# Weight sign by a leaky slope, pinned decay operands, one v tile, gl on GpSimd and fewer early quanta in a fused attention and feed-forward kernel

## The chip, the cores and the metric

The kernel runs on one core of one Trainium2 chip. The metric is the device time of one execution in microseconds (us). The core has TensorE (PE in the profile; PEld is its weight load), VectorE (DVE), ScalarE (ACT), GpSimd (POOL) and SyncE (SP), which here issues every DMA. Each engine works through its own queue in order; semaphores tie the queues together.

## The reference, cut to what matters

```python
scores = scale * np.matmul(q, k.transpose(0, 1, 3, 2))      # 8 batches, 8 heads, 576 tokens, D = 64
cum = np.cumsum(np.log(np.clip(f, 0.0001, 1.0)), axis=-1)
scores = np.where(causal, -1e9, scores + cum[:, :, :, None] - cum[:, :, None, :])
attn = softmax(scores)                                      # with 1e-9 added to the sum
x = np.matmul(attn, v)  # heads side by side: 4608 tokens x 512
h = x @ w_in            # 512 x 2048, float64 weights
g = np.maximum(0.01 * h, h)
out = (g @ w_out).astype(np.float32)
```

So it is causal attention with a forget gate (a decay that is added to the scores), and behind it a feed-forward layer with a leaky ReLU over all 4608 tokens.

## The kernel before, in words

**Precision.** The matmuls of the feed-forward layer and most of the attention run on pairs: a number is rounded to the matmul type (the high part, names ending in h), and the rest is kept as a low part (l). A product is three matmuls: high by high, high by low, low by high.

**Weights.** They lie in memory as float64. `load_weight` (line 157 on) takes one of 16 pieces, 128 partitions by 1024 numbers, as pairs of 32-bit words. ScalarE scales the high word's magnitude with `Abs` (L166); VectorE shifts it left by three (L167), puts the sign back with an AND and an OR (L168), and adds the scaled low word (L172); ScalarE rounds to the high part (L176), VectorE makes the low part (L177). Two raw buffers take turns, and the DMA of piece n+2 is asked for between L172 and L176.

**Early steps.** Before the loop over heads come 13 steps, x = 0 to 12. Twelve of them treat the first 256 tokens of batches 0 to 2, two heads at a time (four steps a batch). `early_scores` makes scores, masked minimum on VectorE (L296 or L326), exponential on ScalarE (L300 or L330) and the scaling by the inverse sum; `early_values` of the step before transposes the weights on PE (tre, L349), copies them by ScalarE (pte, L353) and multiplies by v (ave, L355 and L356). The decays enter the scores by a matmul of `pick`, which selects a head, with `both`, the decays of the two row blocks (L279, L318). `pick` comes from `ident_r`, a copy of the identity. In steps 0 to 3 idle `warm` matmuls on zeros (L114) stand between the scores. WQ says how many weight pieces have been treated by each step: one a step up to step 7, then two. At step 4 (LATER) `later_decays` makes the decays of the full heads (scan L215, L218, L222, ScalarE casts L227, GpSimd subtractions) and writes them to DRAM.

**Quanta.** The feed-forward work is a generator, `ffn`. It goes through 18 groups of 256 tokens. For each group and each of eight weight parts p it makes h (PE, L581, in two halves), g by ScalarE (`Prelu`, L588), gh by VectorE (L594) and gl by VectorE (L595), and one part later the output matmuls (L616, in two halves). Each half is one quantum, so a part has four quanta and a group 32. Groups 0 and 1 are done in two halves of the weights. `fill(n)` takes n quanta from it; it stops where tokens or weight pieces are not there yet. FQ says how many quanta an early step takes. A group's tokens are fetched to `xs`, rounded by VectorE to `xh` and subtracted by GpSimd (helper `minus`, L139), either at part 5 of the group before, if the fetch was made by then, or right where the group begins.

**Heads.** After the early steps, `fix` sets up tiles that stay, and the loop over 64 heads begins: the full 576 tokens of batches 3 to 7, then the rest of batches 0 to 2. In each turn t the head's scores (L425) are interleaved with the transposes (L452) and values (L494) of head t-1 and with fills. `split(t + 1)` makes the next head's operands: ScalarE rounds q and k (L393, L394), GpSimd subtracts for the low parts (s and fixed_m2a or fixed_m2b), VectorE rounds v in two casts (the four full chunks from `vm`, L403; the last 64 tokens from `vt`, L405) and GpSimd subtracts twice for v's low part. A turn's quanta follow from `step = min(have / (left + SLACK), MAXQ) / 8`, with `have` the quanta of ready tokens that are not done, and `left` the turns until more tokens are ready. Behind the heads, the last `fill` does what is left.

**Order.** The code's order is not that of the engines: a scheduler sorts the instructions of each engine by priority and its own estimate of when operands are ready, and lets ready ones overtake. `tc.keep_in_program_order(ins)` adds an edge so that `ins` is queued behind the instruction that was traced before it on its engine; others may still overtake both.

Of the kernel before, what the change touches and what calls it, by code (L numbers as in the profile page):

```python
# [26 lines left out]
GHA = ()  # L27
LATER = 4
ONV = (1, 3)
# [3 lines left out]
ZE = (("z0", "z1", "z2", "z3"), ("vm", "s2b", "m2b", "s2a"))  # L33
FQ = (0, 0, 0, 0, 0, 8, 8, 8, 8, 8, 8, 8, 8)
BUFS = dict(ost=2)
# [7 lines left out]
def forgetting_attention_ffn(ctx, tc, qT, kT, v4, vr, f, w_in, w_out, out):  # L43
# [75 lines left out]
    ident_r = one.tile([P, P], F32R, name="ident_r")  # L119
    nc.vector.tensor_copy(ident_r, eye)  # L120
    ident = ident_r.bitcast(F32)
# [16 lines left out]
    def minus(out, a, b):  # L138
        nc.gpsimd.tensor_tensor(out, a, b, op=ALU.subtract)  # L139
# [17 lines left out]
    def load_weight(n):  # L157

        loaded.append(n)
        _, wh, wl = wpieces[n]  # L160
        wh, wl = (w.rearrange("p c f -> p (c f)") for w in (wh, wl))
        raw = raws.pop(n).rearrange("p m w two -> p (m w) two")
        lo, hi = raw[:, :, 0], raw[:, :, 1]
        t = one.tile([P, 8 * P], I32, tag="vs", name=f"wt_{n}")
        tf = t.bitcast(F32)
        nc.scalar.activation(tf, hi.bitcast(F32), AF.Abs, scale=REBIAS)  # L166
        nc.vector.tensor_scalar(t, t, 3, None, op0=ALU.logical_shift_left)  # L167
        nc.vector.scalar_tensor_tensor(  # L168
            t, hi, -0x80000000, t, op0=ALU.bitwise_and, op1=ALU.bitwise_or
        )  # L170
        low = t.bitcast(U16).rearrange("p (w two) -> p w two", two=2)[:, :, 0]
        nc.vector.scalar_tensor_tensor(  # L172
            low, lo.bitcast(U32), 0.937 * 2.0**-29, low, op0=ALU.mult, op1=ALU.add
        )
        ask(n + 2)
        nc.scalar.copy(wh, tf)  # L176
        nc.vector.tensor_tensor(wl, tf, wh.bitcast(F32), op=ALU.subtract)  # L177
# [8 lines left out]
    pick = one.tile([P, NHEAD], F32R, tag="vt", name="pick")  # L186
    both = one.tile([P, P + T], F32R, tag="kraw", name="both")
    decay_r = [both[:, :P], both[:, P:P + T]]
    bounds = ((0, E), (E, S))

    def decays():
# [7 lines left out]
        )  # L199
        nc.vector.tensor_tensor(pick, ident[:, :NHEAD], ident[:, NHEAD:], op=ALU.add)  # L200
        d = one.tile([P, P + T], F32, tag="z3", name="d")
        for i in range(2):
# [5 lines left out]
        nc.scalar.copy(both, d)  # L208
        nc.vector.tensor_tensor(
            both[NHEAD:], d[NHEAD:], both[NHEAD:].bitcast(F32), op=ALU.subtract  # L210
        )

    def later_decays():

        nc.vector.tensor_tensor_scan(  # L215
            fc[:, E:], fr[:, E:], fr[:, E:], fc[:, E - 1:E], op0=ALU.add, op1=ALU.bypass
        )
        nc.vector.tensor_scalar(fc, fc, -1.0 / SCALE, None, op0=ALU.mult)  # L218
# [16 lines left out]
    def load(t):  # L235
# [8 lines left out]
        if s % 2 == 0:  # L244
            g = s // 2
            nf = min(c1, NFULL)
            vm = one.tile([P, 2, NFULL, D], F32, tag="vm", name=f"vm_{t}")
            nc.sync.dma_start(vm[:, :, :nf], v4[g][:, :, :nf])
            vt = None
            if c1 == NCH:  # L250
                vt = one.tile([REST, 2, D], F32, tag="vt", name=f"vt_{t}")
                nc.sync.dma_start(vt, vr[g])
            pairs[s // 2, c0] = dict(vm=vm, vt=vt)

# [113 lines left out]
    def fix():  # L368
# [11 lines left out]
        vs = fixed["vs"] = one.tile([P, 2, NCH, 2 * D], F32R, tag="vs", name="fixed_vs")  # L380
        nc.gpsimd.memset(vs[:, :, NFULL].bitcast(F32), 0.0)

    def split(t):
# [18 lines left out]
        vs = fixed["vs"][:, o]  # L402
        nc.vector.tensor_copy(vs[:, :NFULL, :D], p["vm"][:, o])  # L403
        minus(vs[:, :NFULL, D:], p["vm"][:, o], vs[:, :NFULL, :D].bitcast(F32))
        nc.vector.tensor_copy(vs[:REST, NFULL, :D], p["vt"][:, o])  # L405
        minus(vs[:REST, NFULL, D:], p["vt"][:, o], vs[:REST, NFULL, :D].bitcast(F32))

# [149 lines left out]
    def ffn():  # L557
# [4 lines left out]
        for at, (n, p0, p1) in enumerate(order):  # L562
# [9 lines left out]
            for p in range(p0, p1):  # L572
# [20 lines left out]
                else:  # L593
                    nc.vector.tensor_copy(gh, g)  # L594
                nc.vector.tensor_tensor(gl, g, gh.bitcast(F32), op=ALU.subtract)  # L595
                yield True
# [39 lines left out]
    quanta = ffn()  # L636
    ready, used, credit = [0], [0], [0.0]

    def fill(n):

        credit[0] += n
        while credit[0] >= 1:
            credit[0] -= 1
            if not next(quanta, None):
                credit[0] = 0
                return
            used[0] += 1
# [22 lines left out]
    ask(1)  # L670
    decays()
    for x, (b, g) in enumerate(steps + [(NE, 0)]):
        if x + 2 < len(steps):
            early_load(*steps[x + 2])
        if x < len(steps):
            early_scores(b, g)
            weights(sum(WQ[:x + 1]))
        if x == LATER:
            later_decays()
        if x:  # L680
            early_values(*steps[x - 1])
            if steps[x - 1][1] == HPB // 2 - 1:
                ready[0] = (steps[x - 1][0] + 1) * T
        fill(FQ[x])
    fix()
    load(0)
    split(0)
    for t in range(nt + 1):
# [25 lines left out]
        if t + 1 < nt:  # L714
            split(t + 1)
        fill(step * (3 - len(spans(t - 1)) if t else 1))
    fill(NG * NQ)

# [33 lines left out]
```

## Time and profile before

| | |
|---|---|
| median of three runs | 1211.28 us (1211.24 to 1211.35) |
| the profiled execution | 1210.85 us |
| its span, first to last instruction | 1209.0 us |
| mean granted TensorE clock | 0.994 |
| busy: PE, DVE, ACT, POOL | 1187.2, 720.5, 610.1, 296.7 us |
| DMA moved | 110.50 MB, mean 91 GB/s |

The profile is of one execution. Its page gives busy time of each engine and groups of instructions by line; other views of the same trace give who waited for whom, the instructions in order of time, the chain of work that ended last, and busy times within stretches that one names. A row of the timeline is start, duration, engine, line, operation, tiles (out<-in), and in brackets the idle time before it and what ended that. A row of the waits is who waited for whom, the sum in us, how often, and the longest. A row of groups ends in busy us, mean ns of one, and the idle time before. PEclk is the share of its full clock that PE was granted.

### The profile page before, as it was taken

Reading aid. Unit: us, or ns where it says so; the run is one execution under the profiler, and the core shown is the slowest. Engines: PE = TensorE matmul, PEld = TensorE weight load, DVE = VectorE, ACT = ScalarE, POOL = GpSimd, SP = SyncE. Lnnn points to the kernel's source line nnn. Section 1 sums busy time; section 2 is a strip of 40 time slices with the busy share of each in tenths; the row PEclk is TensorE's granted clock in tenths of the full one; section 3 lists DMA queues with packets and bytes.
Section 4 is the critical chain, followed back from the end, with each engine's and each line's share of the span. In section 5 each row is a group of like instructions: output and inputs, shape, how many; then the busy total and the mean of one; then the engine's idle time right before and its main releaser. Section 6 shows DMA issues by size and latency. Waiting matters only on the chain.

```text
span 1209.0 us, 21922 instructions
## 1 busy us (share of the span) xinstructions
PE 1187.2 (98%) x7876; PEld 1053.5 (87%) x7876; DVE 720.5 (60%) x1821; ACT 610.1 (50%) x1467; POOL 296.7 (25%) x295
## 2 busy tenths in 40 slices
PE   9899999999999999999999999999999999999998
PEld 6677888898999999999999999999999989888997
DVE  6898767775666666665665555535454666663221
ACT  6775556664565555555554544434434455552111
POOL 0000233332322323232323222223122433330000
PEclk9899999999999999999999999999999999999999
DMA  6544333433233322323232313122213233321000
GB/s 208 180 150 152 117 106 107 124 108 104 80 97 98 115 80 80 98 87 96 70 92 88 115 55 102 38 91 58 83 50 93 76 89 105 91 72 46 19 18 18
DMA packets 69677, 110.50 MB, mean 91 GB/s; under 512 B 10368, under 2 KB 35184, under 8 KB 69568
## 3 DMA queue, kind: packets, MB, share of 16 engines
q1 hardware_dynamic: 69568, 109.09, 29.5%
q8 instruction: 63, 1.03, 0.4%
q14 instruction: 46, 0.38, 0.1%
HBM read 82.62 MB, written 18.56 MB: 84 GB/s over the span
## 4 chain that ended last, share of the span: by engine, by line
PE 90%; DVE 3%; ACT 3%; issue 2%; POOL 1%; DMA 0%; DVEq 0%; ACTq 0%; POOLq 0%
PE h L581 32%; PE o L616 31%; PE sc L425 8%; PE av L494 7%; PE tr L452 7%; PE warm L114 1%; PE ave L355 1%; POOL xs L139 1%; PE tre L349 1%; PE sce L317 1%; ACT wt L166 0%; DVE wt L172 0%; DVE gl L595 0%; PE ave L356 0%; PE sce L287 0%
## 5 line engine op out<-in xcount | busy, mean ns | idle before, releaser
L581 PE MATMUL h<-xh,win_h 128*128 128x256 f32 x1152 | 327.4, 285 | 0.0
L581 PE MATMUL h<-xh,win_l 128*128 128x256 f32 x1152 | 323.6, 281 | 0.4 <-DVE win_l L177 0.4
L581 PE MATMUL h<-xs,win_h 128*128 128x256 f32 x1024 | 287.6, 281 | 5.7 <-POOL xs L139 5.7
L139 POOL TENSOR_TENSOR s<-qraw,s 64x576 fp32r<-64x576 f32 (+1 forms) x64 | 82.0, 1280 | 657.1 <-ACT s L393 597.9
L616 PE MATMUL o<-wout_h,gh 128*128 128x512 f32 x576 | 231.8, 402 | 0.0
L616 PE MATMUL o<-wout_l,gh 128*128 128x512 f32 x576 | 228.6, 397 | 0.0
L616 PE MATMUL o<-wout_h,gl 128*128 128x512 f32 x576 | 227.8, 396 | 0.1
L581 PEld LDWEIGHTS h<-xh,win_h 128*128 128x128 f32 x1152 | 217.5, 189 | 5.6 <-issue 0.5
L581 PEld LDWEIGHTS h<-xh,win_l 128*128 128x128 f32 x1152 | 217.2, 189 | 0.7 <-DVE win_l L177 0.6
L581 PEld LDWEIGHTS h<-xs,win_h 128*128 128x128 f32 x1024 | 193.2, 189 | 10.5 <-POOL xs L139 7.0
L588 ACT ACTIVATE g<-h 128x512 f32<-128x512 f32 x144 | 85.9, 597 | 226.9 <-PE h L581 225.0
L465 ACT CAST ph<-tr 128x128 fp32r<-128x128 f32 (+2 forms) x272 | 121.7, 450 | 133.3 <-PE tr L452 129.8
L594 DVE CAST gh<-g 128x512 fp32r<-128x512 f32 x144 | 74.9, 520 | 188.6 <-ACT g L588 186.0
L467 DVE TENSOR_TENSOR pl<-tr,ph 128x128 fp32r<-128x128 f32 (+2 forms) x272 | 138.4, 516 | 31.3 <-ACT ph L465 30.8
L616 PEld LDWEIGHTS o<-wout_h,gl 128*128 128x128 f32 x576 | 108.2, 188 | 25.6 <-issue 0.5
L425 PE MATMUL sc<-m,s 128*128 128x128 f32 (+2 forms) x336 | 121.8, 367 | 1.8 <-POOL s L139 1.5
L616 PEld LDWEIGHTS o<-wout_h,gh 128*128 128x128 f32 x576 | 108.4, 188 | 16.8 <-DVE ql L273 0.2
L616 PEld LDWEIGHTS o<-wout_l,gh 128*128 128x128 f32 x576 | 108.5, 188 | 16.1
L436 ACT ACTIVATE fixed_z<-fixed_z,max 96x480 f32<-96x480 f32 (+1 forms) x128 | 94.3, 736 | 46.2 <-DVE max L430 44.7
L430 DVE CUSTOM_DVE_ANT_0 z<-sc,tri 128x128 f32<-128x128 f32 (+1 forms) x144 | 63.4, 443 | 88.9 <-PE sc L425 88.1
L430 DVE CUSTOM_DVE_ANT_0 fixed_z<-sc,tri 96x480 f32<-96x480 f32 (+1 forms) x128 | 70.4, 550 | 63.2 <-PE sc L425 62.2
L595 DVE TENSOR_TENSOR gl<-g,gh 128x512 fp32r<-128x512 f32 x144 | 102.3, 710 | 3.1
(131 smaller groups left out, 1871.1 us busy)
## 6 DMA issues: line engine op xcount, KB each, us to landing
kraw<-in_kT SPq DMA_DIRECT2D x128, 144.0 KB
qraw<-in_qT SPq DMA_DIRECT2D x80, 144.0 KB
wraw<-in_w_in SPq DMA_DIRECT2D x16, 512.0 KB
wraw<-in_w_out SPq DMA_DIRECT2D x16, 512.0 KB
vm<-in_v SPq DMA_DIRECT2D x32, 256.0 KB
xs<-xd SPq DMA_DIRECT2D x16, 512.0 KB
out<-ost SPq DMA_DIRECT2D x28, 256.0 KB
rb<-inv SPq DMA_DIRECT2D x40, 144.0 KB
```

What stands on the lines that cost most here:

```text
L139: nc.gpsimd.tensor_tensor(out, a, b, op=ALU.subtract)
L425: nc.tensor.matmul(ps[:m, :b - a], h["s" + w][:, cols], h["m" + w][:, a:b], start=y == 0, stop=y == 1,)
L430: nc.vector.tensor_tensor_reduce(out=z[:, a:b], in0=ps[:m, :b - a], in1=tri[:m, at:at + b - a], scale=-SCALE, scalar=3.0e38 if x == 0 else ...
L436: nc.scalar.activation(z, z, AF.Exp, bias=h["max"][:m, last:last + 1], scale=-1.0, accum_out=fixed["sum" + "ab"[s // 2 % 2]][:m, i, s % 2: ...
L452: nc.tensor.transpose(ps[:, x * m:(x + 1) * m], z[:m, j * P:(j + 1) * P], ident[:m, :m])
L465: nc.scalar.copy(o, src)
L467: nc.vector.tensor_tensor(o, src, hi.bitcast(F32), op=ALU.subtract)
L494: nc.tensor.matmul(ps[:, a - lo:hi - lo], fixed["vs"][:, odd, j, :], h[w][:, at:at + hi - a], start=(n == 0), stop=(n == len(steps) - 1),)
L581: nc.tensor.matmul(ph[:, e, :], w[:, c, fs], xx[:, c, :], start=(c == 0 and x == 0), stop=(c == NCC - 1 and x == 2),)
L588: nc.scalar.activation(g, ph, AF.Prelu, alpha=0.01)
L595: nc.vector.tensor_tensor(gl, g, gh.bitcast(F32), op=ALU.subtract)
L616: nc.tensor.matmul(acc[k], gg[:, e, ts], w[:, e, :], start=(fc_ == 2 * p0 and x == 0), stop=(fc_ == 2 * p1 - 1 and x == 2),)
```

## The change

It has five parts.

- The sign: `Abs` becomes `Prelu` with slope -(2^32) for negative numbers. A negative number thus gets a positive result whose exponent is 32 higher, and the shift by three moves that bit to the place of the sign. The AND and OR (L168) goes.
- The decays: the copy to `ident_r`, `pick` (now traced ahead of `decays`), the subtraction into `both` and the scan of the later decays are kept in program order. `later_decays` comes at step 0 instead of 4.
- Step 4: the values of step 3 are traced ahead of the scores of step 4, not behind.
- v: `vm` is one tile that stays, with five chunks, the last one zero below the 64 tokens; ScalarE rounds all of it in one copy, GpSimd subtracts once.
- Quanta: the early steps 5 to 8 take 4 and steps 9 to 12 take 5, instead of 8. In the loop over heads gl is made by GpSimd instead of VectorE; before and behind it stays on VectorE.

```diff
-LATER = 4
+LATER = 0
+FIRST = (4,)
...
-FQ = (0, 0, 0, 0, 0, 8, 8, 8, 8, 8, 8, 8, 8)
+FQ = (0, 0, 0, 0, 0, 4, 4, 4, 4, 5, 5, 5, 5)
...
-    nc.vector.tensor_copy(ident_r, eye)
+    tc.keep_in_program_order(nc.vector.tensor_copy(ident_r, eye))
...
-        nc.scalar.activation(tf, hi.bitcast(F32), AF.Abs, scale=REBIAS)
+        nc.scalar.activation(tf, hi.bitcast(F32), AF.Prelu, scale=REBIAS, alpha=-(2.0**32))
         nc.vector.tensor_scalar(t, t, 3, None, op0=ALU.logical_shift_left)
-        nc.vector.scalar_tensor_tensor(
-            t, hi, -0x80000000, t, op0=ALU.bitwise_and, op1=ALU.bitwise_or
-        )
...
+    tc.keep_in_program_order(
+        nc.vector.tensor_tensor(pick, ident[:, :NHEAD], ident[:, NHEAD:], op=ALU.add)
+    )
...
-        nc.vector.tensor_tensor(pick, ident[:, :NHEAD], ident[:, NHEAD:], op=ALU.add)
...
-        nc.vector.tensor_tensor(
+        tc.keep_in_program_order(nc.vector.tensor_tensor(
             both[NHEAD:], d[NHEAD:], both[NHEAD:].bitcast(F32), op=ALU.subtract
-        )
+        ))
...
-        nc.vector.tensor_tensor_scan(
+        tc.keep_in_program_order(nc.vector.tensor_tensor_scan(
             fc[:, E:], fr[:, E:], fr[:, E:], fc[:, E - 1:E], op0=ALU.add, op1=ALU.bypass
-        )
+        ))
...
-            nf = min(c1, NFULL)
-            vm = one.tile([P, 2, NFULL, D], F32, tag="vm", name=f"vm_{t}")
-            nc.sync.dma_start(vm[:, :, :nf], v4[g][:, :, :nf])
-            vt = None
-            if c1 == NCH:
-                vt = one.tile([REST, 2, D], F32, tag="vt", name=f"vt_{t}")
-                nc.sync.dma_start(vt, vr[g])
-            pairs[s // 2, c0] = dict(vm=vm, vt=vt)
+            vm = fixed["vm"]
+            nc.sync.dma_start(vm[:, :, :NFULL], v4[g])
+            nc.sync.dma_start(vm[:REST, :, NFULL], vr[g])
+            pairs[s // 2, c0] = dict(vm=vm)
...
-        nc.gpsimd.memset(vs[:, :, NFULL].bitcast(F32), 0.0)
+        vm = fixed["vm"] = one.tile([P, 2, NCH, D], F32, tag="vm", name="fixed_vm")
+        nc.gpsimd.memset(vm[:, :, NFULL], 0.0)
...
-        nc.vector.tensor_copy(vs[:, :NFULL, :D], p["vm"][:, o])
-        minus(vs[:, :NFULL, D:], p["vm"][:, o], vs[:, :NFULL, :D].bitcast(F32))
-        nc.vector.tensor_copy(vs[:REST, NFULL, :D], p["vt"][:, o])
-        minus(vs[:REST, NFULL, D:], p["vt"][:, o], vs[:REST, NFULL, :D].bitcast(F32))
+        nc.scalar.copy(vs[:, :, :D], p["vm"][:, o])
+        minus(vs[:, :, D:], p["vm"][:, o], vs[:, :, :D].bitcast(F32))
...
-                nc.vector.tensor_tensor(gl, g, gh.bitcast(F32), op=ALU.subtract)
+                if beside[0]:
+                    minus(gl, g, gh.bitcast(F32))
+                else:
+                    nc.vector.tensor_tensor(gl, g, gh.bitcast(F32), op=ALU.subtract)
...
+    def values_of(x):
+
+        if x:
+            early_values(*steps[x - 1])
+            if steps[x - 1][1] == HPB // 2 - 1:
+                ready[0] = (steps[x - 1][0] + 1) * T
+
     for x, (b, g) in enumerate(steps + [(NE, 0)]):
         if x + 2 < len(steps):
             early_load(*steps[x + 2])
+        if x in FIRST:
+            values_of(x)
         if x < len(steps):
             early_scores(b, g)
             weights(sum(WQ[:x + 1]))
         if x == LATER:
             later_decays()
-        if x:
-            early_values(*steps[x - 1])
-            if steps[x - 1][1] == HPB // 2 - 1:
-                ready[0] = (steps[x - 1][0] + 1) * T
+        if x not in FIRST:
+            values_of(x)
         fill(FQ[x])
     fix()
+    beside[0] = True
...
+    beside[0] = False
     fill(NG * NQ)
```

More of the change, by code (lines that the diff above doesn't have):

```diff
@@ L636, in forgetting_attention_ffn @@
     quanta = ffn()
-    ready, used, credit = [0], [0], [0.0]
+    ready, used, credit, beside = [0], [0], [0.0], [False]
     def fill(n):
```

## The prediction

> **What bounds the kernel now.** I read the page first, then the waits of TensorE (PE), then busy time by stage, then the timeline where a stage lost time.
>
> ```profile
> span 1209.0 us, 21922 instructions
> PE 1187.2 (98%) x7876; PEld 1053.5 (87%) x7876; DVE 720.5 (60%) x1821; ACT 610.1 (50%) x1467; POOL 296.7 (25%) x295
> ```
>
> PE is busy for 1187.2 of 1209.0 us and its matmuls stay the same in kind and number, so the change can win only from the 21.8 us in which PE stands still, from stretches at a lowered clock, and from latency hidden under the idle `warm` matmuls of the first steps. The waits that cost most, then the stages:
>
> ```profile
> PE h L581 <- POOL xs L139: 5.7, 4, 1.9
> PE ave L355 <- ACT pte L353: 5.5, 4, 2.0
> ```
>
> ```profile
> core 0: us, PE busy (x) PEld busy (x) DVE busy (x) ACT busy (x) POOL busy (x), PEclk, DMA share, GB/s
> 0.00:42.65 42.65, 40.64 (x179) 26.86 (x179) 29.14 (x90) 29.25 (x69) 3.24 (x12) 1.00 0.58 197
> 42.65:54.02 11.37, 7.71 (x31) 4.95 (x31) 9.12 (x13) 6.97 (x18) 1.19 (x1) 0.55 0.65 198
> 54.02:87.40 33.38, 32.80 (x215) 25.89 (x213) 31.15 (x78) 25.00 (x63) 0.00 (x0) 1.00 0.47 159
> 87.40:136.50 49.10, 47.56 (x311) 38.73 (x310) 41.14 (x77) 31.10 (x66) 1.93 (x2) 1.00 0.45 155
> 164.40:270.00 105.60, 100.01 (x678) 87.92 (x676) 78.29 (x225) 70.81 (x187) 39.69 (x37) 1.00 0.37 110
> 270.00:300.00 30.00, 28.05 (x179) 25.30 (x178) 18.12 (x45) 13.55 (x36) 8.87 (x8) 0.94 0.37 110
> 300.00:1060.00 760.00, 758.71 (x5189) 691.11 (x5188) 450.33 (x1169) 389.89 (x943) 219.72 (x210) 1.00 0.29 85
> ```
>
> Three places lose time: the first four early steps up to 42.65 us, where PE is kept busy by `warm`; the turn into step 4 (42.65 to 54.02), with 3.66 us of PE idle and a mean clock of 0.55; and the first nine heads (164.4 to 270), with 5.59 us idle. From 300 to 1060 us only 1.29 us is to be had: there a relieved VectorE gains nothing, and a slower gl can only lose.
>
> **The change part by part.** The sum is against the profiled execution, 1210.85 us (span 1209.0 and 1.85 around it); the median of the runs, 1211.28, is 0.43 more.
>
> *Decay operands pinned.*
>
> ```profile
> 7.18 0.88 DVE L215 TENSOR_TENSOR_SCAN fc<-fr,fc 128x320 f32<-128x320 f32 x1
> 8.10 0.46 DVE L218 TENSOR_SCALAR fc<-fc 128x576 f32<-128x576 f32 x1
> 8.59 0.56 DVE L209 TENSOR_TENSOR both<-d,both 64x384 fp32r<-64x384 f32 x1
> 9.16 1.04 DVE L222 TENSOR_SCALAR start<-fc 128x128 f32<-128x128 f32 x5
> 10.11 0.22 DVE L120 CAST ident_r<-eye 128x128 fp32r<-128x128 f32 x1
> 10.36 0.23 DVE L200 TENSOR_TENSOR pick<-ident_r 128x64 fp32r<-128x64 f32 x1
> ```
>
> The scheduler had floated the later decays (L215, L218, L222: 2.38 us) in front of `both` and `pick`, which the first decay matmul needs. The pin on L215 sends them behind piece 0's weights, so `pick` can be done about 2.1 us sooner. But ScalarE gates the first exponentials too:
>
> ```profile
> 9.71 1.15 ACT L166 ACTIVATE wt<-wraw 128x1024 f32<-128x1024 f32 x1 [1.90 <-DMA wraw<-in_w_in]
> 10.88 1.28 ACT L330 ACT_TABLE_LOAD   x1
> 12.17 0.40 ACT L330 ACTIVATE ze<-ze,maxe 128x128 f32<-128x128 f32 x1
> ```
>
> The exponential stands behind the first weight piece, which waited for its DMA, and a table load. If that order stays, almost nothing is won; if the earlier scores let it overtake, up to 2.1. I take -1.0 (0 to -2.1).
>
> *Sign by the slope.* ScalarE's L166 stays one pass; the VectorE pass L168 goes.
>
> ```profile
> L595 DVE TENSOR_TENSOR gl<-g,gh 128x512 fp32r<-128x512 f32 x144 | 102.3, 710 | 3.1
> ...
> L168 DVE SCALAR_TENSOR_TENSOR wt<-wraw,wt 128x1024 int32<-128x1024 int32 x16 | 19.8, 1236 | 0.3
> ```
>
> Of sixteen times 1.24 us, only the three or so in steps 0 to 3 lie on a chain that is not covered by PE work: 3 x 1.24 = 3.7 at most; VectorE is 68% busy there (29.14 of 42.65), so I count 60%: -2.2 (0 to -3.7). The other pieces lie beside matmuls and make room for what follows.
>
> *Later decays at step 0.* Their 2.38 us of VectorE land between steps 0 and 1, along with two ScalarE casts and two GpSimd subtractions that stood at step 4:
>
> ```profile
> 40.23 0.66 ACT L227 CAST fck<-fc 128x576 fp32r<-128x576 f32 x1
> 40.79 0.67 ACT L227 CAST fcq<-start 128x576 fp32r<-128x576 f32 x1
> 41.37 1.13 ACT L166 ACTIVATE wt<-wraw 128x1024 f32<-128x1024 f32 x1
> 42.40 0.39 ACT L300 ACTIVATE ze<-ze,maxe 128x128 f32<-128x128 f32 x1
> ...
> 44.15 0.46 ACT L353 COPY pte<-tre 128x384 f32<-128x384 f32 x1
> ```
>
> 2.38 + 1.33 = 3.7 us if all of it stood on the chain; the engines have idle time there, so +1.2 (0 to +3.7). The four decay DMAs move with them, on SP ahead of the q, k and v loads of step 3, which are not needed for two steps: nothing, unless SP waits there longer than a step.
>
> *Step 3's values ahead of step 4's scores.* The rows above show the fault: the transposed weights of step 3 are copied (44.15) only behind the decay casts, a weight piece and four exponentials of step 4. PE waits for that copy 2.00 us and for the second one 1.66, with 7.71 us of work at half clock behind it, about 3.5 us: 3.66 + 3.5 = 7.1 in all. With the values first, and the casts gone to step 0, the copy can run about when L227 does now. Something new comes late: step 4's own exponentials, one copy later. I take -5.0 (0 to -7.1). The Trainium skill (TensorE: Matmul & The Clock Gate, Part 1) puts the fall to half clock after about one idle window of 3.4 us; by that, gaps of 2.0 and 1.7 us would keep the clock, the stretch would be worth 3.66, and taken alike (2.6 for 5.0) the sum would be -4.3. The trace differs: mean clock 0.55 with no gap over 2.0. The row decides.
>
> *Fewer quanta in the early steps.* A quantum of feed-forward work is 1.40 us:
>
> ```profile
> 108.30 2.80 PE h L581 x24
> ```
>
> (24 matmuls, two quanta.) By the loop, steps 5 to 12 now do 8+2+4+8+8+8+8+8 = 54 quanta (step 6 stops for a weight piece, step 7 for the second batch's tokens); after, 4x4 + 4x5 = 36. The 18 x 1.40 = 25 us of matmuls only move. In 87.40:136.50, three steps, a step takes 15.9 us of PE, 13.7 of VectorE, 10.4 of ScalarE. After: PE 15.9 - 3 x 1.40 = 11.7; VectorE 13.7 less two L168 (2.5) and three quarters of a gh and gl (0.8) = 10.4; ScalarE about 9.9. PE is still longest, but the margin shrinks from 2.2 to 1.3 us, and the DMA rate rises from 155 GB/s to about 155 x 16.4/11.9 = 214, near the 197 held up to 42 us. PE idle in 54 to 136.5 was 2.1 us; I add +1.5 (0 to +6).
>
> *The same quanta in the first heads.* have/(left + SLACK) rises from (96-54)/12 = 3.5 to (96-36)/12 = 5.0 quanta a head. Of the 5.59 us idle of that stage 1.3 is the wait for the split of token group 2, which comes right at its need before and after; 4.3 are short waits that more matmuls can cover. -2.0 (-4.3 to +1).
>
> *gl on GpSimd, v in one tile.* About 116 gl move. Their price on GpSimd lies between these two shapes:
>
> ```profile
> L139 POOL TENSOR_TENSOR fixed_m2a<-kraw,m 64x576 fp32r<-64x576 f32 x32 | 45.7, 1427 | 2.5 <-POOL s L139 0.2
> L139 POOL TENSOR_TENSOR xs<-xs,xh 128x1024 fp32r<-128x1024 f32 x16 | 38.2, 2388 | 92.0 <-DVE xh L553 92.0
> ```
>
> 1.43 - 64 x (2.39 - 1.43)/448 = 1.29 us, 0.6 more than on VectorE. PE wants gl four quanta after the h it came from, 5.6 us and the attention between: covered. Without that cover each costs 0.6. Behind a gl on GpSimd wait s, m2 and vs of the next head, and xs of the next group. Groups 2, 3, 15 and 16 are split right at their need in both versions (the four waits of 5.7 us above stay); three of them can get a gl in front, 1.29 each. +0.8 (-1 to +4). v's rounding moves from two VectorE casts to one ScalarE copy of 128x320, less than the 0.46 us of the 128x384 copy above, and saves one GpSimd instruction a head: both engines wait for PE there, 0.
>
> Sum: -1.0 - 2.2 + 1.2 - 5.0 + 1.5 - 2.0 + 0.8 = -6.7: 1204.15 for the profiled execution, 1204.5 by the median.
>
> **The rivals.**
>
> *A, more of it:* the copy stall, the clock and the short waits go whole (-7.1 and -4.3 for -5.0 and -2.0), L168 counts fully (-3.7): -12.6, 1198.7. For it: PE is the bound everywhere else. Against: chains that lose one link mostly show the next.
>
> *B, slower:* the early steps lose their cover. Steps 8 to 11 have three engines within 2 us of each other and 18 quanta less in hand. If VectorE is busy only 80% of a step there (9.12 of 11.37, as in the turn to step 4), a step takes 10.4/0.80 = 13.0, 1.3 us of idle, 5.2 in four; two falls of the clock like the one at 43 us add 2 x 3.5. 12.2 in place of 1.5: +4.0, 1215.3. It decides from 8.2 us of idle and lost clock in steps 5 to 12. Against: the scheduler fetches later matmuls forward into gaps, as here, h of step 5 in the midst of step 3:
>
> ```profile
> 32.82 0.71 PE h L581 x6
> ```
>
> *C, GpSimd gates the heads:* in the first heads its results come just in time, and it holds VectorE up.
>
> ```profile
> 235.30 1.47 POOL L139 TENSOR_TENSOR fixed_m2b<-kraw,m 64x576 fp32r<-64x576 f32 x1
> ```
>
> ```profile
> 236.82 0.33 PE L425 MATMUL sc<-fixed_m2b,fixed_s2b 128*128 128x128 f32 x1
> ```
>
> ```profile
> 604.41 1.27 DVE L594 CAST gh<-g 128x512 fp32r<-128x512 f32 x1 [1.42 <-ACT g L588]
> ...
> 611.72 0.42 DVE L594 CAST gh<-g 128x512 fp32r<-128x512 f32 x1
> ```
>
> m2b ended 0.05 us ahead of its matmul; a cast took 1.27 us for 0.42 with a GpSimd subtraction beside it. A gl in front in half of nine heads and of three xs: 6 x 1.29 = 7.7 for 0.8: +0.2, 1211.5. Against: 1.5 quanta more a head give 2.1 us. The Trainium skill (GPSIMD Engine Reference, Engine selection) speaks against this move: two-input elementwise work is put on VectorE, GpSimd being about twice as slow; 1.29 against 0.71 here agrees.
>
> *D, the stall only moves:* the pins set a lower bound for an instruction, not an upper, and the order is the scheduler's; step 4's scores come late by what step 3's values gain. Without -5.0: -1.7, 1209.6.
>
> **How the numbers follow.** Forecast 0.56, A 0.12, D 0.13, B 0.11, C 0.08. About 0.2%, 2.4 us, is what a measurement can tell from no change. Faster: forecast and A, 0.68; same: D and 0.03 of C, 0.16; slower: B and the rest of C, 0.16. The range runs from A's 1198 to 1212, past D and C; it leaves out B and the far end of A.
>
> **What would show it.** Right: `pick` done by about 8.5 us; no wait of ave for pte over 1 us near 40 us and the clock at 1.00 there; step 4 begun before 40 us; main heads beginning about 25 to 30 us earlier; PE idle under 4 us in the first nine heads; xs still waited for four times. Wrong: half clock in steps 5 to 12, PE idle over 8 us there (B), or PE waits for s, m2 or gl on POOL in many heads (C).

## The result, and the profile after

| | before | after |
|---|---|---|
| median of four runs | 1211.26 us (1209.85 to 1211.35) | 1197.24 us (1196.73 to 1197.86) |
| the profiled execution | 1210.85 us | 1197.86 us |
| its span | 1209.0 us | 1196.1 us |

The ratio of the two is 0.9887 (95% interval 0.9870 to 0.9904): 14.0 us faster. The forecast was 6.8 us faster, and the range ended at 1198. The direction was right; the gain is twice the forecast.

First the page of after, its span and its busy times:

```profile
span 1196.1 us, 21843 instructions
PE 1178.5 (99%) x7876; PEld 1050.5 (88%) x7876; DVE 581.3 (49%) x1561; ACT 636.2 (53%) x1531; POOL 436.6 (36%) x347
```

PE does the same 7876 matmuls, but its busy time fell too, from 1187.2 to 1178.5 us. So of the 12.9 us of span only 4.2 are PE's idle time (21.8 to 17.6); the other 8.7 lie inside the time that counts as busy. Before has two stretches at half clock ahead of its end, from 43.78 and from 275.88 us, and after has none; PE is busy for 7.70 and 3.41 us in them:

```profile
43.78:54.02 10.24, 7.70 (x30) 4.95 (x31) 8.00 (x13) 5.84 (x12) 0.06 (x1) 0.50 0.66 197
```

Half of 11.11 us is 5.6, so some 3 of the 8.7 us are something else. The waits of PE in after (who waited for whom, us in all, times, longest):

```profile
PE h L576 <- POOL xs L140: 4.6, 4, 1.3
PE ave L351 <- ACT pte L349: 3.5, 8, 1.4
PE av L489 <- DVE pl L462: 2.3, 4, 1.7
```

The waits for `xs` are still four, but the longest is 1.3 us instead of 1.9. To see the rest by stage, both traces are cut at the same instructions: the reciprocal that ends step 3, the third cast of q (step 6's), the second head's cast `s`, those of the eleventh and of the thirteenth head. First after, then before:

```profile
core 0: us, PE busy (x) PEld busy (x) DVE busy (x) ACT busy (x) POOL busy (x), PEclk, DMA share, GB/s
0.00:35.00 35.00, 33.54 (x141) 22.30 (x141) 24.43 (x73) 26.23 (x62) 4.45 (x12) 1.00 0.68 227
35.00:48.00 13.00, 12.31 (x88) 9.40 (x88) 10.55 (x25) 10.61 (x25) 0.00 (x0) 1.00 0.65 216
133.60:251.70 118.10, 114.23 (x789) 103.24 (x788) 68.84 (x198) 75.04 (x195) 51.20 (x39) 1.00 0.36 106
251.70:284.20 32.50, 31.46 (x213) 28.01 (x212) 16.08 (x47) 18.31 (x48) 15.44 (x11) 1.00 0.36 107
```

```profile
38.00:53.30 15.30, 11.23 (x58) 7.59 (x57) 11.94 (x25) 10.59 (x24) 2.81 (x2) 0.69 0.66 208
164.40:267.30 102.90, 97.31 (x657) 85.28 (x656) 76.61 (x218) 68.26 (x183) 37.78 (x35) 1.00 0.38 111
267.30:302.20 34.90, 32.95 (x212) 29.87 (x212) 21.05 (x55) 17.93 (x46) 10.78 (x9) 0.95 0.34 100
```

In after no stage has a lowered clock. But the stages hold different quanta, so their lengths can't be compared as they stand. A ledger can: from the time that has gone by at each cut, take what PE would need at the dense pace for the matmuls done so far, without `warm`. The pace is that of the 24 h matmuls of 256 columns in 2.80 us that the prediction quotes, 116.7 ns each or 0.456 ns a column. What is left is lost time, whether idle, slow or at half clock:

| stage, up to | lost before | lost after | difference | terms of the forecast |
|---|---|---|---|---|
| end of step 3 (38.0; 35.0 us) | 29.5 | 27.2 | -2.3 | -1.0 - 2.2 + 1.2 = -2.0 |
| third cast of q (53.3; 48.0) | 10.0 | 4.7 | -5.3 | -5.0 |
| second head (164.4; 133.6) | 16.3 | 17.3 | +1.0 | +1.5 |
| eleventh head (267.3; 251.7) | 20.6 | 15.9 | -4.7 | -2.0 |
| thirteenth head (302.2; 284.2) | 6.2 | 3.6 | -2.6 | none |
| the end | 63.8 | 64.8 | +1.0 | +0.8 |
| all | 146.4 | 133.5 | -12.9 | -6.7 |

So each of the three early stages came out within half a us of its terms, together -6.6 for -5.5, and the forecast failed between 133 and 284 us. Two cautions. The kernel with gl on VectorE throughout (below), whose edit takes hold only in the heads, ends step 3 at 36.0 us where after has 35.0, so one execution gives that stage to about 1 us. And the profiled execution of after, the slowest of its four, has a wait of its own in the stage up to the eleventh head:

```profile
172.79 0.96 PE L489 MATMUL av<-pl,fixed_vs 128*128 128x448 f32 x5 [1.75 <-DVE pl L462]
```

VectorE had stood idle for 1.73 us there, until the DMA of `rb` came. Three kernels below that differ from after only ahead of the heads (values behind scores, late decays, no pins) don't have this wait and lose 13.9 to 14.0 us in this stage, for 15.9. The timeline of after shows the early part, and the end of the last weight piece ahead of the first heads:

```profile
8.79 0.23 DVE L187 TENSOR_TENSOR pick<-ident_r 128x64 fp32r<-128x64 f32 x1
10.23 1.12 ACT L167 ACTIVATE wt<-wraw 128x1024 f32<-128x1024 f32 x1 [2.33 <-DMA wraw<-in_w_in]
12.67 0.40 ACT L326 ACTIVATE ze<-ze,maxe 128x128 f32<-128x128 f32 x1
...
38.64 0.48 ACT L349 COPY pte<-tre 128x384 f32<-128x384 f32 x1 [0.16 <-PE tre L345]
40.60 0.48 ACT L349 COPY pte<-tre 128x384 f32<-128x384 f32 x1 [0.54 <-PE tre L345]
43.35 0.39 ACT L296 ACTIVATE ze<-ze,maxe 128x128 f32<-128x128 f32 x1
...
125.11 2.00 DVE L175 TENSOR_TENSOR wout_l<-wt,wout_h 128x1024 fp32r<-128x1024 f32 x1 [0.84 <-ACT wout_h L174]
133.58 0.67 ACT L390 CAST s<-qraw 128x576 fp32r<-128x576 f32 x1 [0.20 <-PE sc L420]
```

`pick` is made 1.57 us earlier than before (8.79 for 10.36), but the first exponential is not (12.67 for 12.17): it still stands behind the first weight piece and its DMA. The copies of step 3 now wait only for their transposes and run ahead of step 4's exponentials. The last weight piece ends at 127.11 us; the first matmul of a head's scores starts at 127.55, and the last row is the second head's cast. In before they stood further apart: 146.02 and 159.53 us.

### The profile page after: what moved, and what is told of

Its sections match the earlier page's. It is cut to its first block, busy times and chain, and to the rows that moved or that the text cites. A ratio compares the mean times of both kernels' runs of the same rounds, so it can differ in the third digit from the quotient of the medians.

```text
span 1196.1 us, 21843 instructions
## 1 busy us (share of the span) xinstructions
PE 1178.5 (99%) x7876; PEld 1050.5 (88%) x7876; DVE 581.3 (49%) x1561; ACT 636.2 (53%) x1531; POOL 436.6 (36%) x347
## 4 chain that ended last, share of the span: by engine, by line
PE 89%; DVE 4%; ACT 3%; issue 2%; POOL 1%; DMA 0%; SPq 0%; DVEq 0%; ACTq 0%; POOLq 0%
PE h L576 32%; PE o L614 31%; PE av L489 8%; PE sc L420 8%; PE tr L447 6%; PE warm L115 1%; DVE wt L170 1%; POOL xs L140 1%; PE ave L351 1%; PE sce L313 1%; ACT ze L296 1%; ACT wt L167 1%; PE tre L345 0%; DVE fixed_z L425 0%; DMA rb<-inv 0%
## 5 line engine op out<-in xcount | busy, mean ns | idle before, releaser
L140 POOL TENSOR_TENSOR gl<-g,gh 128x512 fp32r<-128x512 f32 x116 | 150.3, 1296 | 319.7 <-DVE gh L589 297.1
L589 DVE CAST gh<-g 128x512 fp32r<-128x512 f32 x144 | 80.2, 557 | 218.1 <-ACT g L583 214.8
L140 POOL TENSOR_TENSOR s<-qraw,s 64x576 fp32r<-64x576 f32 (+1 forms) x64 | 78.9, 1233 | 268.2 <-ACT s L390 264.9
```

## The experiments

Times are medians; differences are against after (1197.24 us) where the kernel starts from after, against the kernel before of the same call (1210.1 to 1211.1) where it starts from before. Medians of the kernel before differ by about 1 us between calls, so a difference of less than 1 us is not read. Ledger numbers are from one profiled execution each.

**The turn into step 4.** Three kernels undo one part each.

```diff
-FIRST = (4,)
+FIRST = ()
```

> The changed kernel with the values of step 3 again traced behind the scores of step 4. Theory 1 (the order of the two decides the turn into step 4): the copy of the transposed weights stands behind four exponentials again, PE waits 2 to 4 us and may fall to half clock: +3 to +7, 1200 to 1204 us. Rival (the casts of the later decays and the missing VectorE pass already free the copy; the order is the scheduler's anyway): under 1 us, 1197 to 1198 us.

1199.25 us, +2.0. The stall of before is back, once, in the timeline and in the windows that answer to it:

```profile
44.34 0.45 ACT L349 COPY pte<-tre 128x384 f32<-128x384 f32 x1
44.84 0.65 PE L351 MATMUL ave<-pte,ve 128*64 128x256 f32 x2 [1.73 <-ACT pte L349]
```

```profile
42.54:45.95 3.41, 1.68 (x8) 0.84 (x7) 2.92 (x8) 3.41 (x12) 0.00 (x0) 1.00 0.48 157
45.95:49.37 3.42, 3.29 (x21) 3.06 (x20) 3.42 (x14) 2.80 (x8) 0.00 (x0) 0.50 0.60 199
```

The copy stands behind four exponentials of step 4 again, and 3.4 us at half clock follow. The mechanism is the one of the prediction; undone alone it costs 2.0 us, where the prediction's 5.0 took in the decay casts that go to step 0 as well.

```diff
-LATER = 0
+LATER = 4
```

> The changed kernel with the later decays at step 4 again (their scan still pinned, now behind step 4's weights on VectorE). Theory 1 (values first is what frees the copy): the casts and GpSimd subtractions fall into the turn again but behind the copy, and 2.4 us of VectorE leave steps 0 and 1: between -1 and +1.5, 1196 to 1199 us. Rival (the casts in the turn are half of the stall): +2 to +5, 1199 to 1202 us.

1205.98 us (1205.26 to 1209.36), +8.7, more than either theory gave. The timeline says why:

```profile
52.12 0.67 ACT L227 CAST fck<-fc 128x576 fp32r<-128x576 f32 x1
52.81 2.06 SPq L230 DMA_DIRECT2D dec_k<-fck  x2
54.64 0.68 ACT L227 CAST fcq<-start 128x576 fp32r<-128x576 f32 x1 [1.85 <-DVE start L222]
55.35 2.25 SPq L230 DMA_DIRECT2D dec_q<-fcq  x2
56.88 0.61 ACT L268 CAST qh<-qk 128x512 fp32r<-128x512 f32 x1
60.77 0.47 PE L283 MATMUL sce<-qh,ql 64*128 64x128 f32 x2 [2.89 <-DVE ql L269]
```

The second early cast of q (L268, step 5's) comes at 56.88 us, where after has it at 45.10, and 13.65 us at half clock follow from 58.66. The rounded decays lie in two of the buffers that `qh` and `ql` use next; the cast can't write there until the DMAs have read them. Two more kernels test that. The first leaves out only the pin on the scan as well, so that the scheduler may float the later decays:

```diff
-        tc.keep_in_program_order(nc.vector.tensor_tensor_scan(
+        nc.vector.tensor_tensor_scan(
...
```

> The changed kernel with the later decays at step 4 and their scan not pinned. Theory 1 (at step 4 the rounded decays take the two slots that step 5 needs for its high and low parts of q and k, and are given back only by the DMA to DRAM; the pin puts the scan behind step 4's weights and so makes that late): with the scan floating, the slots come back as early as in the kernel before, step 5's cast starts near 45 us, and 3 to 6 of the 8.7 us that the late pinned decays cost come back: 1200 to 1203 us, with pick late again as scan and start stand ahead of it. Rival (the casts and GpSimd subtractions in the turn cost it, wherever the scan stands): 1204.5 to 1206.5 us.

1203.84 us, +6.6: 2.1 of the 8.7 came back, which settles nothing. The second keeps the decays late and pinned but gives them other room (the last half pair of `wout`, idle until the last weight piece):

```diff
-        for name, tag, x, to in (("fck", "s1", fc, dec_k), ("fcq", "m1", start, dec_q)):
-            r = one.tile([P, S], F32R, tag=tag, name=name)
+        for spare, _, x, to in ((wout_h, 0, fc, dec_k), (wout_l, 0, start, dec_q)):
+            r = spare[-1].rearrange("p c f -> p (c f)")[:, :S]
```

> The kernel after, with the later decays made in step 4 as in the kernel before, but rounded into the weights' last half pair, which is idle until the last weight piece, and so not into the two slots that step 5's casts of q need. Theory (the late decays cost 8.7 us because their slots are held until their DMAs have read them, and step 5's casts wait for that): no cast of step 5 is late, the half-clock stretch of 13.7 us from 58.7 us is gone, 1198 to 1200.5 us. Rival (the work of the late decays on ScalarE and GpSimd itself is what delays step 5): 1203 to 1206 us, with the cast again at 55 us or later.

1200.10 us, +2.9. The decays' DMAs are as late as in the kernel above (first start 52.7 us), and no cast of q waits; by source line and by the timeline:

```profile
L230 SPq DMA_DIRECT2D dec_k<-wout_h x2: 484/492/499, 52.7 to 54.3; - x2
```

```profile
39.03 0.63 ACT L268 CAST qh<-qk 128x512 fp32r<-128x512 f32 x1
47.30 0.62 ACT L268 CAST qh<-qk 128x512 fp32r<-128x512 f32 x1
```

Its clock is full throughout. So 5.9 of the 8.7 us are the shared buffers, not the work of the late decays. In the kernel before, where the scan isn't pinned, those casts ran at 40.23 us and step 5's cast of q came at 45.02, after 0.41 us of waiting for the decays' DMA. Since without the pin the late place still costs 6.6 us in after, the price depends on the other parts of the change too; which of them was not separated.

Without any of the four pins, `pick` in its old place:

```diff
-    tc.keep_in_program_order(nc.vector.tensor_copy(ident_r, eye))
+    nc.vector.tensor_copy(ident_r, eye)
-    tc.keep_in_program_order(
-        nc.vector.tensor_tensor(pick, ident[:, :NHEAD], ident[:, NHEAD:], op=ALU.add)
-    )
...
+        nc.vector.tensor_tensor(pick, ident[:, :NHEAD], ident[:, NHEAD:], op=ALU.add)
...
-        tc.keep_in_program_order(nc.vector.tensor_tensor(
+        nc.vector.tensor_tensor(
             both[NHEAD:], d[NHEAD:], both[NHEAD:].bitcast(F32), op=ALU.subtract
-        ))
+        )
...
-        tc.keep_in_program_order(nc.vector.tensor_tensor_scan(
+        nc.vector.tensor_tensor_scan(
...
```

> The changed kernel without the four edges of program order and with pick traced in its old place. Theory 1 (ScalarE's wait for the first weight piece and its table load set the first exponential): 0 to +1, 1197 to 1198 us. Rival (the order of decays ahead of pick costs its 2.4 us): +2 to +2.5, 1199 to 1200 us.

1200.62 us, +3.4, more than either theory gave. PE waits 1.27 us for `pick` at 11.97 us, and the waits for the copies `pte` rise from 3.5 to 5.2 us. The ledger is 3.2 us worse at the end of step 3.

**Quanta, sign and the first heads.**

```diff
-FQ = (0, 0, 0, 0, 0, 4, 4, 4, 4, 5, 5, 5, 5)
+FQ = (0, 0, 0, 0, 0, 8, 8, 8, 8, 8, 8, 8, 8)
```

> The changed kernel with the old quanta of the early steps (8 each), all else as changed. Theory 1 (more matmuls in the first nine heads cover their short waits): the nine heads lose again what they won, about 4 us, the early steps win back about 1, and the wait for xs of group 3 may again lower the clock (up to 2.5): 1200 to 1203 us. Rival (VectorE's relief did it: gl, v and sign gone from its queue): 1196 to 1198 us, and the nine heads stay short of idle time.

1203.86 us, +6.6; by the ledger +1.6 up to the second head, +4.2 to the eleventh, +1.3 at the next token group. In the heads PE waits for s again (1.7 us, with 3.4 us at half clock behind it), and the longest wait for `xs` is 2.1:

```profile
PE h L576 <- POOL xs L140: 5.9, 4, 2.1
PE sc L420 <- POOL s L140: 1.7, 1, 1.7
```

The new quanta are thus needed for what the forecast missed in the heads. But by themselves, in the kernel before:

```diff
-FQ = (0, 0, 0, 0, 0, 8, 8, 8, 8, 8, 8, 8, 8)
+FQ = (0, 0, 0, 0, 0, 4, 4, 4, 4, 5, 5, 5, 5)
```

> The kernel before with the new quanta of the early steps alone. Theory 1: the nine heads win 3 to 4.5 us, the early steps lose 2 to 4 as VectorE (12.9 us a step) now outlasts PE (11.7): 1208 to 1211 us. Rival (fewer quanta pay only with a relieved VectorE): 1212 to 1216 us.

1208.55 us (1207.13 to 1210.73; the profiled execution 1210.30) against 1210.27, -1.7 (ratio 0.9989, 0.9980 to 0.9998). The sign by a pass of VectorE, put back in after:

```diff
-        nc.scalar.activation(tf, hi.bitcast(F32), AF.Prelu, scale=REBIAS, alpha=-(2.0**32))
+        nc.scalar.activation(tf, hi.bitcast(F32), AF.Abs, scale=REBIAS)
         nc.vector.tensor_scalar(t, t, 3, None, op0=ALU.logical_shift_left)
+        nc.vector.scalar_tensor_tensor(
+            t, hi, -0x80000000, t, op0=ALU.bitwise_and, op1=ALU.bitwise_or
+        )
```

> The changed kernel with the sign put back by the VectorE pass, sixteen times 1.24 us. Theory 1: about 2 us in steps 0 to 3, and 1 to 4 in the early steps 5 to 12, where VectorE comes to 12.9 us of work beside 11.7 of PE: +3 to +6, 1200 to 1203 us. Rival (the pass lies in gaps of VectorE): under 1 us, 1197 to 1198 us.

1206.04 us, +8.8, beyond both theories. By the ledger 1.6 of it is lost by the second head, 5.1 more by the sixth and 1.6 by the eleventh. The leaky slope alone in the kernel before:

```diff
-        nc.scalar.activation(tf, hi.bitcast(F32), AF.Abs, scale=REBIAS)
+        nc.scalar.activation(tf, hi.bitcast(F32), AF.Prelu, scale=REBIAS, alpha=-(2.0**32))
         nc.vector.tensor_scalar(t, t, 3, None, op0=ALU.logical_shift_left)
-        nc.vector.scalar_tensor_tensor(
-            t, hi, -0x80000000, t, op0=ALU.bitwise_and, op1=ALU.bitwise_or
-        )
```

> The kernel before with the sign by the slope alone, 8 quanta an early step. Theory 1 (the pass pays only where VectorE outlasts PE; with 8 quanta PE has 15.9 us a step and VectorE 13.7): 2 to 3 us from steps 0 to 3, 1207 to 1208.5 us. Rival (the 8.8 us that the pass costs in the changed kernel are its own worth): 1201 to 1203 us.

1213.71 us against 1211.09, +2.6: by itself it makes the kernel slower (ratio 1.0028, 1.0015 to 1.0040); both theories failed. The waits for the copies `pte` are 7.7 us there, 5.5 before, and the ledger of its profiled execution loses 2.0 us more in the turn into step 4 and 1.8 up to the second head. And these last two diffs (new quanta and slope) together in the kernel before:

> The kernel before with the sign by the slope and the new quanta, nothing else. Theory 1 (fewer quanta need a VectorE that keeps pace, so the two pay more together than apart): more than the sum of the two alone, 1202 to 1205 us. Rival (they add): the sum of what the new quanta alone (1.7 us) and the sign alone give, about 1205.5 to 1207 us.

1204.64 us, -6.45. Apart they make +0.9, together -6.45: 7.3 us exist only when both are there. Where the last weight piece ends shows why:

| kernel | last weight piece done | first score of a head | second head's cast |
|---|---|---|---|
| before | 146.0 us | 159.5 | 164.4 |
| before, new quanta | 151.2 | 134.6 | 143.8 |
| before, new quanta and slope | 127.1 | 134.5 | 140.5 |
| after | 127.1 | 127.6 | 133.6 |
| after, sign by VectorE | 144.9 | 128.4 | 138.0 |
| the same, six quanta more (below) | 142.5 | 136.2 | 144.1 |

From the timelines of the second and of the third row:

```profile
143.81 0.66 ACT L393 CAST s<-qraw 128x576 fp32r<-128x576 f32 x1
149.94 1.21 DVE L177 TENSOR_TENSOR wout_l<-wt,wout_h 128x1024 fp32r<-128x1024 f32 x1
```

```profile
125.85 1.23 DVE L174 TENSOR_TENSOR wout_l<-wt,wout_h 128x1024 fp32r<-128x1024 f32 x1 [1.11 <-ACT wout_h L173]
140.54 0.67 ACT L390 CAST s<-qraw 128x576 fp32r<-128x576 f32 x1 [0.25 <-PE sc L422]
```

Fewer early quanta bring the heads forward by some 25 us, and with the pass of VectorE the weights aren't ready by then: their last piece falls among the operands of the first heads. After with the pass put back shows the collision itself:

```profile
138.03 0.66 ACT L393 CAST s<-qraw 128x576 fp32r<-128x576 f32 x1
138.76 2.23 POOL L140 TENSOR_TENSOR s<-qraw,s 64x576 fp32r<-64x576 f32 x1 [11.07 <-ACT s L393]
139.76 2.45 DVE L173 SCALAR_TENSOR_TENSOR wt<-wraw,wt 128x1024 uint16<-128x1024 uint32 x1
141.06 2.75 POOL L140 TENSOR_TENSOR fixed_m2b<-kraw,m 64x576 fp32r<-64x576 f32 x1
143.34 1.56 DVE L178 TENSOR_TENSOR wout_l<-wt,wout_h 128x1024 fp32r<-128x1024 f32 x1 [0.28 <-ACT wout_h L177]
```

s and m2b take 2.23 and 2.75 us for the usual 1.43, L173 2.45 for 1.36, and PE waits in the first heads:

```profile
PE sc L423 <- DMA fixed_s2a<-s: 3.3, 1, 3.3
PE sc L423 <- POOL s L140: 1.5, 1, 1.5
```

If the collision is the cause, and not VectorE's time as such, more matmuls between the weights and the heads must cure it. The kernel with the pass, with six quanta more in the last early step:

```diff
-FQ = (0, 0, 0, 0, 0, 4, 4, 4, 4, 5, 5, 5, 5)
+FQ = (0, 0, 0, 0, 0, 4, 4, 4, 4, 5, 5, 5, 11)
```

> The kernel after, with the sign of the weights by a pass of VectorE as in the kernel before, and the last early step given 11 quanta where it has 5, so that TensorE has some 8 us more work of its own before the first head. Theory (the pass costs 8.8 us because the last weight pieces end inside the first heads): the waits at the first heads (1.49 at 141.0 us, 3.31 at 155.9 us) and the fall of the clock at 156.3 us are gone, 1199 to 1202 us. Rival (the pass costs VectorE's time in the heads, wherever the pieces lie): no more than 1 us comes back, 1205 to 1207 us.

1200.02 us: 6.0 of the 8.8 came back with every pass of VectorE still there. What the six quanta give in after without the pass was not run. The wait of 3.3 us and the half clock are gone, one of 1.4 for s is left. In its timeline, the last piece now ends ahead of the cast:

```profile
141.26 1.23 DVE L178 TENSOR_TENSOR wout_l<-wt,wout_h 128x1024 fp32r<-128x1024 f32 x1 [0.32 <-ACT wout_h L177]
144.12 0.66 ACT L393 CAST s<-qraw 128x576 fp32r<-128x576 f32 x1
```

**gl and v.** gl by VectorE throughout:

```diff
     fix()
-    beside[0] = True
```

> The changed kernel with gl on VectorE throughout. Theory 1: gl on GpSimd buys nothing and costs about 1 us behind 300 us, so 1196 to 1197 us. Rival (relief of VectorE paid in the first nine heads): those heads lose 2 to 3 us, 1198.5 to 1200 us.

1197.40 us, +0.2: moving 116 subtractions to GpSimd changes nothing that can be measured. v in its two tiles, rounded by VectorE, as before:

```diff
...
-        nc.scalar.copy(vs[:, :, :D], p["vm"][:, o])
-        minus(vs[:, :, D:], p["vm"][:, o], vs[:, :, :D].bitcast(F32))
+        nc.vector.tensor_copy(vs[:, :NFULL, :D], p["vm"][:, o])
+        minus(vs[:, :NFULL, D:], p["vm"][:, o], vs[:, :NFULL, :D].bitcast(F32))
+        nc.vector.tensor_copy(vs[:REST, NFULL, :D], p["vt"][:, o])
+        minus(vs[:REST, NFULL, D:], p["vt"][:, o], vs[:REST, NFULL, :D].bitcast(F32))
```

> The changed kernel with v in its two old tiles, rounded by two VectorE casts. Theory 1: nothing beyond 0.7 us either way, 1196.5 to 1198 us. Rival (relief): 1 to 2 us in the first nine heads, 1198 to 1199.5 us.

1199.47 us, +2.2, the rival's size and stage. By the ledger it is lost between the sixth and the eleventh head (+2.4 us): the wait for `xs` of token group 2 is 3.1 us long there, and 3.4 us at half clock follow. Why that split comes later there was not followed up.

**The four late splits.** In after, the waits for `xs` are the largest that are left. A token group that was fetched late misses the one part at which it could be split ahead. One comparison changes that:

```diff
-                if p == p1 - AHEAD and at + 1 < len(order):
+                if p >= p1 - AHEAD and at + 1 < len(order):
```

> The changed kernel in which a token group is also split ahead when its fetch was made after part 5 (any part from 5 on, not 5 alone). Theory 1 (the four waits for xs and its VectorE cast, 5.4 us, stand at the need only for that test): the waits go whole, 1191 to 1193.5 us. Rival (GpSimd's work ahead of time delays s, m2 and gl of the heads, or PE waits elsewhere): 1195 to 1198 us.

1189.44 us (1189.12 to 1190.90), ratio to before 0.9827 (0.9813 to 0.9842): 7.8 us less than after, and better than both theories. It beats both kernels. All four waits are gone, and nothing has taken their place. In after they came to 5.4 us with the one for `xh`; what the rest of the 7.8 us is was not followed up.

```profile
PE ave L351 <- ACT pte L349: 3.6, 9, 1.4
PE av L489 <- DVE pl L462: 0.6, 3, 0.3
```

The same edit in the kernel before:

> The kernel before, with the one comparison changed by which the token groups that are fetched late are split ahead as well. Theory (the four waits for xs are a fault of the order alone, independent of this change, and cost some 1.4 to 2 us each with the clock they take): they are gone, and it is 5 to 9 us faster than the kernel before, 1202 to 1206 us. Rival (before this change VectorE and GpSimd have no room for the split beside the heads): other waits stand in their place, 1207 to 1211 us.

1207.12 us, -3.0, less than the theory gave: three waits go, but the one of token group 3 stays, 1.92 us. There that group's tokens are fetched at 264.3 us and needed at 276.2, so the next part at which it can be split is right at the need. In after with the edit they are fetched at 243.4 us and split at 252.3, and PE needs them only at 262.6. So the waits are a fault of the order, and yet what their cure is worth depends on how far the heads run ahead, and that this change moved.

## Why the prediction was wrong

**Right.** The chain of step 4 as found in before: the copies behind casts, a weight piece and exponentials (step 3 to the third cast of q: -5.3 for -5.0). The early steps (+1.0 for +1.5), the late part (+1.0 for +0.8), gl. Of "what would show it" these came: no wait over 1 us near 40 us and full clock there, 3.87 us of PE idle in nine heads (118.10 - 114.23), four waits for `xs`. Heads began 32 us earlier (127.55 for 159.53), where 25 to 30 were said, and `pick` was done at 9.0 us, not at about 8.5. That step 4 began before 40 us tells nothing: its first scores from the rounded q start at 38.48 us, and in before at 34.90.

**Right in part by luck: the first four steps**, -2.3 for -2.0. By the ledger of that stage, each to about 1 us, undoing the sign costs 2.1 us (2.2 in the sum) and undoing the pins 3.2 (1.0); the decays back at step 4 make it 2.0 us longer, where the sum had their move to step 0 cost 1.2. So two of three terms were off, and the sum hides it.

**Wrong by size: the quanta in the first nine heads**, "-2.0 (-4.3 to +1)", measured -4.7, past the end of its range. The step that failed is the bound: it took the 5.59 us in which PE was idle for all that more matmuls could win. PE's idle time fell only by 1.7 us (5.59 to 3.87). The 3.87 us of after hold the 1.75 us for `pl`; without that wait the stage would be at about -6.5, still with 3 us that no idle time explains. The ledger's other 3.0 us were inside "busy": of the 97.31 busy us of before, 82.3 would do for its matmuls at the dense pace, 15.0 were slow; in after 12.0 of 114.23, though the stage has more work. That the quanta do it is shown both ways: the new quanta alone take the slow part of before from 15.0 to 12.6 us, and the old ones take that of after from 12.0 to 13.3 (both without the 1.7 us that a fall to half clock adds to this stage in these two kernels). Of the 4.2 us that the old quanta cost after in this stage, 1.1 are idle time, 1.7 the half clock, and the rest slow. What the prediction did not see at all is its condition: only with the sign pass gone are the weights ready before the heads that the quanta bring forward (the table above). It priced the sign pass beyond step 3 at nothing, since those pieces "lie beside matmuls"; in after it is worth 8.8 us. The same holds for the later decays: priced at +1.2, worth 8.7 where they are.

**Wrong by omission: the turn of token group 3**, counted as unchanged ("the four waits of 5.7 us above stay"), measured -2.6. They do stay, but this one is 1.04 us instead of 1.95, by the timelines of before and of after, and keeps the clock:

```profile
275.32 0.38 PE L581 MATMUL h<-xs,win_h 128*128 128x256 f32 x1 [1.95 <-POOL xs L139]
```

```profile
267.57 0.39 PE L576 MATMUL h<-xs,win_h 128*128 128x256 f32 x1 [1.04 <-POOL xs L140]
```

0.9 of idle, and half of 3.41 us at half clock, 1.7, make 2.6. The prediction's own table had the mark of it, a clock of 0.94 from 270 to 300 us, but that stretch isn't among its three places that lose time. The four kernels with the old quanta (before, after with them, before with the slope, before with the early split) wait 1.9 to 2.1 us there; those with the new ones 1.03 to 1.12, except the kernel in which the wait is gone. The part that did it is the quanta, shown in both directions.

**The parts interlock.** Undone one at a time, they cost 6.6 + 0.2 + 2.2 + 2.0 + 8.7 + 8.8 + 3.4 = 31.9 us, over twice the 14.0 that all of them gained. Rival A, "more of it", named the right direction at 1198.7, with a chance of only 0.12, and the wrong place: its gain lay in the sign of steps 0 to 3 and in the copy's stall, which both came out as in the sum. Its third term, -4.3 for the short waits of the heads, is near the -4.7 in size, but short waits gave only 1.7 of it. Of the rivals that end higher, none of what they wait for came: no half clock in the early steps (B), no wait for s, m2 or gl in the heads (C), and the stall did not move (D), since the engines kept the traced order there.

What stays open: why v's old form makes the split of group 2 late; why the slope alone makes the early steps of the kernel before slower; and between which matmuls the slow part of PE's busy time lies, since the ledger shows only that it shrinks with more quanta. Two slips of the prediction change nothing: half of its 7.71 us at half clock is 3.9 us and not 3.5, and 6.7 less than 1211.28 is 1204.6.

## What to carry to other kernels

Bound what more dense work can win by the lost time against the dense pace, not by idle time: here PE's busy time held 15.0 us of loss in a stage that showed 5.6 us of idle time. Before moving a stage forward, look at what it will meet there (the last weight piece, a buffer that a DMA still reads), since an edit can pay only when another has cleared the place; test parts together as well as apart. And a wait that the change leaves alone deserves a look of its own: here one comparison was worth 7.8 us.

## What the runs showed of the hardware

**The clock falls by windows, and a short wait is enough.** Clock changes in each trace lie a whole number of 3.413 us apart (in before the falls at 43.78 and 275.88 us, 232.1 or 68 x 3.413). Inside the kernels a fall came at the end of a window in which PE was busy for 0.10 to 0.57 of it; the lowest that kept the clock was 0.48. Two waits of the kernel after with the old quanta, 1.72 and 2.12 us long:

```profile
159.89:163.30 3.41, 1.69 (x11) 1.22 (x10) 1.14 (x5) 1.84 (x6) 3.24 (x3) 1.00 0.21 47
163.30:166.72 3.42, 3.42 (x14) 2.85 (x13) 0.61 (x3) 0.09 (x1) 0.82 (x1) 0.50 0.62 173
269.12:272.54 3.42, 1.84 (x15) 1.84 (x16) 0.33 (x1) 0.41 (x2) 1.53 (x1) 1.00 0.44 143
272.54:275.95 3.41, 3.41 (x25) 3.04 (x24) 0.86 (x3) 1.83 (x5) 0.98 (x1) 1.00 0.00 0
```

The shorter wait cost the clock (busy 1.69 of 3.41), the longer one did not (1.84 of 3.42). It depends on where the wait and its neighbours fall in the window, so the price of the same wait differs by 1.7 us between kernels. In before a window with 1.89 of 3.42 fell too, so the limit is near a half; it isn't sharper by these numbers, in which the ends of matmuls are modelled. The Trainium skill (TensorE: Matmul & The Clock Gate, Part 1) has the free-running window of 3413 ns, with which the trace agrees, and the fall after one idle window; none of the windows ahead of these falls was wholly idle, and a wait of 1.7 us was enough.

**VectorE and GpSimd slow each other.** Beyond the rows of the collision above, the five instructions of L222 took 2.21 us in after, from 18.52 us on, where they took 1.04 in before. By source line, in after:

```profile
L222 DVE TENSOR_SCALAR start<-fc x5: 264/278/1443, 18.5 to 19.3; 128x128 f32<-128x128 f32 x3, 128x96 f32<-128x96 f32 x2
```

Only the last one is long, 1443 ns. It starts at 19.29 us, just behind a GpSimd subtraction (19.25 to 20.66 us), and ends at 20.73, 0.07 us behind it: it looks held until the subtraction was through, rather than slowed throughout. The Trainium skill (GPSIMD Engine Reference, Specifications) says that the two share their SBUF interfaces, with contention for some VectorE instructions; the stretched rows agree, on both engines at once.
